# Other batches and other rows for the scattered dV stores of an attention backward kernel

## The chip, the core and the metric

The kernel runs on one core of a Trainium2 chip. The metric is the device time in microseconds (us) of one execution, as the median of several. The core has five engines that compute or issue (TensorE, here PE; VectorE, DVE; ScalarE, ACT; GpSimd, POOL; SyncE, SP) and sixteen DMA engines that move data between the core's memory and the device's. "Engine 4" and the like below always means one of these sixteen.

## The reference

Forward and backward pass of grouped-query attention: 32 batches, 32 query heads, 4 key/value heads, 4 query positions, 2048 keys, head size 128, bfloat16. Returned are the output and the gradients of q, k and v.

```python
B, Hq, Hkv, Sq, Sk, D = 32, 32, 4, 4, 2048, 128

def _fwd_reference(q, k, v):
    k = jnp.repeat(k, Hq // Hkv, axis=1)
    v = jnp.repeat(v, Hq // Hkv, axis=1)
    scores = jnp.einsum("bhqd,bhkd->bhqk", q, k) * D ** -0.5
    p = _softmax(scores, axis=-1)
    return jnp.einsum("bhqk,bhkd->bhqd", p, v)

def reference(q, k, v, grad_out):
    out, vjp = jax.vjp(_fwd_reference, q, k, v)
    return (out, *vjp(grad_out))
```

## The kernel before

One batch is one step of work: 4 heads of keys times 32 query rows (8 query heads by 4 positions) fill the 128 partitions. K, V, dK and dV of a batch are each held in two tiles ("rows") of 128 partitions by 4096 elements, two heads in each; K's tiles and the second tiles of the outputs are 128 elements longer, for q, grad_out, the output and dq. There are 20 such tiles (slots), which loads and stores share.

The whole order of work is written out by hand in the text `PLAN`: four characters name a unit (which operation, which part, where, which tile), and `emit` turns each unit into instructions in that order; nothing reorders them. Within a batch: loads of K and V (L245), transposes of them on PE (L260) and copies out of PSUM by ACT or DVE (L226, L228), scores (L274), minimum and exponential (L279, L283), dop on POOL (L290), transposes of the probabilities, output (L312) and dV (L334) on PE, its copies to the slots (L340), then dP, dS, dQ and dK in the same way. Batches overlap in the plan.

SP issues every plain load (L245) and store (L350; the last pieces of batch 31 L346) in the plan's order. A plain transfer of 128 rows puts 8 rows on each of the 16 DMA engines; each row is one packet of 8192 or 8448 bytes.

Five of the 32 stores of dV's first tile go another way. For a batch in `SPREAD` (L23) SP leaves the store out (L349), and POOL issues it as indirect DMAs ("scatter", L201), in pieces of rows (`PIECES`, L24). This stands behind qp of the next batch (L291 to L299). An indirect DMA of n rows uses as many engines as the largest divisor of n up to 16, one engine after the other from where the last indirect DMA left off: 2 rows lie on two engines, 126 on fourteen with nine rows each. A store of 3 words at the start (L205) moves that place to engine 3, so the 2 rows fall on engines 3 and 4 and the 126 on all the others; 13 words after the last batch (L299) bring it round to 0. Every piece has an output tensor of its own, and the host puts the pieces into dV.

The slot of a scattered tile is written again by the dV copies of batch b+2 (L340).

Of the kernel before, what the change touches and what calls it, by code (L numbers as in the profile page):

```python
# [16 lines left out]
ROW = 2 * 16 * P  # L17
# [2 lines left out]
SLOTS, E_TILES, DS_TILES = 20, 2, 2  # L20
TILES = dict(KT=8, VT=7, ET=2, DT=2)

SPREAD = (4, 6, 8, 10, 12)  # L23
PIECES = ((126, 2), (0, 126))  # L24

NAMES = dict(
    a="LK", b="LV", c="QT", d="QTe", e="KT", f="KTe", g="VT", h="VTe", i="S", j="MX", k="EX", l="RC", m="dop", n="qp",
# [141 lines left out]
def kernel(  # L169
# [8 lines left out]
    dv0: bass.AP,  # L178
    dv1: bass.AP,
    spread,  # L180
    turns,
):
    nc = tc.nc
    B, D, C = k0.shape[0], P, 16
# [13 lines left out]
    at = const_pool.tile([P, 1], mybir.dt.int32, name="at")  # L198
    nc.gpsimd.iota(at[:], pattern=[[0, 1]], base=0, channel_multiplier=1)

    def scatter(out, in_):  # L201
        nc.gpsimd.indirect_dma_start(out=out, in_=in_, in_offset=None,
                                     out_offset=bass.IndirectOffsetOnAxis(ap=at[0:in_.shape[0], 0:1], axis=0))

    scatter(turns[0], at[0:3, 0:1])  # L205
    junk = const_pool.tile([P, D], BF16, name="junk")
    slots = [const_pool.tile([P, LONG], BF16, name=f"row{i}") for i in range(SLOTS)]
    tiles = {x: [const_pool.tile([P, 8 * P], BF16, name=f"{x.lower()}_sb{i}") for i in range(n)]
# [6 lines left out]
    T = collections.defaultdict(dict)  # L215
# [17 lines left out]
    def emit(u):  # L233
# [12 lines left out]
        elif name == "QT":  # L246
            ps = t["qtp"] = bank(u)[:, 0:P]
            for j, x in enumerate(("q", "go")):
                nc.tensor.transpose(out=ps.bitcast(BF16)[:, P * j:P * j + P], in_=t[x], identity=ident[:])  # L249
        elif name == "QTe":  # L250
            t["qdt"] = sm_pool.tile([P, 2 * P], BF16, name="qdt_sb", bufs=3)
            copy16(u.where, t["qdt"][:], t["qtp"])
        elif name in ("KT", "VT", "ET", "DT"):
            x, (half, h) = name[0], divmod(i, NH) if name in ("KT", "VT") else (i, None)
            t[name, i] = tiles[name][u.tile]
            ps = t[name + "p", i] = bank(u)
            src = t[x, h] if h is not None else t["e" if x == "E" else "ds"][:]
            src = src.bitcast(FP32).rearrange("p (j d) -> p j d", d=P)
            for j in range(4):
                nc.tensor.transpose(out=ps[:, P * j:P * j + P], in_=src[:, 4 * half + j, :], identity=ident32[:])  # L260
        elif name in ("KTe", "VTe", "ETe", "DTe"):
            copy16(u.where, t[name[:2], i][:], t[name[:2] + "p", i])
        elif name in ("S", "DP"):
            if name == "S" and i == 0:
                t["S"], t["e"] = bank(u, 4), e_sb[u.tile]
            if name == "DP":
                t["DP", i] = bank(u, 2)
                if i == 0:
                    t["ds"] = ds_sb[u.tile]
            out = t["S"][:, 2 * QW * i:2 * QW * i + 2 * QW] if name == "S" else t["DP", i]  # L270
            x, side = ("KT", 0) if name == "S" else ("VT", 1)
            for w in range(2):
                for h, r in enumerate(rows):
                    nc.tensor.matmul(out[r, QW * w:QW * w + QW], lhsT=t["qdt"][:, P * side + 32 * h:P * side + 32 * h + 32],  # L274
                                     rhs=t[x, NH * i + h][:, QW * w:QW * w + QW],
                                     start=True, stop=True, tile_position=(0, 32 * h))
        elif name == "MX":
            t["m"] = sm_pool.tile([P, 1], FP32, name="m")
            nc.vector.tensor_scalar(out=t["e"][:], in0=t["S"], scalar1=-scale, scalar2=None, op0=ALU.mult,  # L279
                                    op1=ALU.min, accum_out=t["m"][:])  # L280
        elif name == "EX":
            t["l"] = sm_pool.tile([P, 1], FP32, name="l")
            nc.scalar.activation(out=t["e"][:], in_=t["S"], func=ACT.Exp, bias=t["m"][:], scale=scale,  # L283
                                 accum_out=t["l"][:])
        elif name == "RC":
            t["rinv"] = sm_pool.tile([P, 1], FP32, name="rinv")
            nc.vector.reciprocal(out=t["rinv"][:], in_=t["l"][:])  # L287
        elif name == "dop":
            t["dop"] = sm_pool.tile([P, D], BF16, name="dop_sb", bufs=2)
            nc.gpsimd.tensor_scalar(out=t["dop"][:], in0=t["go"], scalar1=t["rinv"][:], scalar2=None, op0=ALU.mult)  # L290
        elif name == "qp":  # L291
            t["qp"] = sm_pool.tile([P, D], BF16, name="qp_sb", bufs=2)
            nc.gpsimd.tensor_scalar(out=t["qp"][:], in0=t["q"], scalar1=t["rinv"][:], scalar2=scale, op0=ALU.mult,
                                    op1=ALU.mult)
            if b - 1 in SPREAD:
                for (first, count), piece in zip(PIECES, spread[SPREAD.index(b - 1)]):
                    scatter(piece, T[b - 1]["DV", "out", 0][first:first + count, 0:ROW])
                if b - 1 == SPREAD[-1]:
                    scatter(turns[1], at[0:13, 0:1])  # L299
        elif name == "rs":  # L300
            t["rs"] = sm_pool.tile([P, 1], FP32, name="rs")
            nc.gpsimd.tensor_scalar(out=t["rs"][:], in0=t["rinv"][:], scalar1=scale, scalar2=None, op0=ALU.mult)
        elif name in ("O", "DQ"):
            if i == 0:
                t[name] = bank(u)[:, 0:D]
            xt, x = ("ET", "V") if name == "O" else ("DT", "K")
            left = t[xt, i][:].rearrange("p (j q e) -> p j q e", q=P, e=2)
            for c in range(8):
                j, odd = divmod(c, 2)
                for h, r in enumerate(rows):  # L310
                    right = t[x, h].rearrange("p (j d e) -> p j d e", d=D, e=2)
                    nc.tensor.matmul(t[name][r, :], lhsT=left[:, j, r, odd], rhs=right[:, 4 * i + j, :, odd],  # L312
                                     start=(i == 0 and c == 0), stop=(i == 1 and c == 7), tile_position=(0, 32 * h))
        elif name in ("Oe", "DQe"):
            x, by, to = ("o", "rinv", "DV") if name == "Oe" else ("dq", "rs", "DK")
            t[x] = t[to, "out", 1][:, ROW:LONG]
            if u.where == "A":
                nc.scalar.activation(out=t[x], in_=t[name[:-1]], func=ACT.Copy, scale=t[by][:])
            else:
                nc.vector.tensor_scalar(out=t[x], in0=t[name[:-1]], scalar1=t[by][:], scalar2=None, op0=ALU.mult)  # L320
        elif name == "DL":
            t["dl"] = sm_pool.tile([P, 1], FP32, name="delta")
            nc.vector.tensor_tensor_reduce(out=junk[:], in0=t["o"], in1=t["go"], scale=1.0, scalar=0.0,
                                           op0=ALU.mult, op1=ALU.add, accum_out=t["dl"][:])
        elif name == "DS":
            w = slice(2 * QW * i, 2 * QW * i + 2 * QW)
            nc.vector.scalar_tensor_tensor(out=t["ds"][:, w], in0=t["DP", i], scalar=t["dl"][:], in1=t["e"][:, w],  # L327
                                           op0=ALU.subtract, op1=ALU.mult)
        elif name in ("DV", "DK"):
            i, g = divmod(i, 2)  # L330
            acc = t[name, i, g] = bank(u, 2)
            moving, still = ("e", "dop") if name == "DV" else ("ds", "qp")
            for h in (2 * g, 2 * g + 1):
                nc.tensor.matmul(acc[:, QW * (h % 2):QW * (h % 2) + QW], lhsT=t[still][rows[h], :],  # L334
                                 rhs=t[moving][rows[h], QW * i:QW * i + QW], start=True, stop=True,
                                 tile_position=(32 * h, 0))
        elif name in ("DVe", "DKe"):
            i, g = divmod(i, 2)
            copy = nc.scalar.copy if u.where == "A" else nc.vector.tensor_copy
            copy(out=heads_of(t[name[:2], "out", g])[:, :, QW * i:QW * i + QW],  # L340
                 in_=t[name[:2], i, g].rearrange("p (h c) -> p h c", h=2))
        elif name == "SK" and i in LAST:
            g, first, runs, n = LAST[i]
            part = lambda row: (row[:, 0:ROW].rearrange("p (h c) -> p h c", h=2)[:, :, first:first + n] if runs == 2
                                else row[:, first:first + n])
            nc.sync.dma_start(out=part(dk_r[g][b]), in_=part(t["DK", "out", g]))  # L346
        elif name in ("SV", "SK"):
            n = LONG if i else ROW
            if not (name == "SV" and i == 0 and b in SPREAD):  # L349
                nc.sync.dma_start(out=(dv_r if name == "SV" else dk_r)[i][b], in_=t["D" + name[1], "out", i][:, 0:n])  # L350
# [48 lines left out]
```

## Time and profile before

| what | before |
|---|---|
| time, median of 3 runs | 668.98 us (667.71 to 670.45) |
| the profiled execution | 667.87 us, its span 665.2 us |
| busy: PE, DVE, ACT, POOL | 605.3, 570.6, 568.6, 51.0 us |
| data moved | 273.96 MB in 38652 packets, 412 GB/s over the span |
| share of the DMA engines' time | SP's queue 96.6%, POOL's 1.9%, instruction fetch 0.6% and 0.1% |
| POOL's indirect DMAs | 10 of rows, 2 of words; issue 0.86 to 1.05 us each |
| scatter, from issue to landing | 5.6 to 12.1 us, median 9.3 |

The span runs from the first to the last instruction. Busy time is that of the engine itself. A DMA is seen in two ways: as an instruction that issues it, and as packets that the sixteen engines move; "landing" is the last of the 16 increments of its semaphore. q1 is SP's queue, q0 POOL's, q8 and q14 fetch instructions.

### The profile page before, as it was taken

To read this page: it belongs to the slowest core of one execution; us is meant where nothing else is said; L and a number is where in the kernel's file an instruction comes from. 1 tells how busy PE (TensorE), PEld (TensorE's weight loads), DVE (VectorE), ACT (ScalarE), POOL (GpSimd) and SP (SyncE) were. 2 spreads that over 40 slices of the span, in tenths; PEclk is the share of its full clock that TensorE was granted. 3 is DMA by queue.
4 is the path that set the end of the run, shared out by engine and by line. 5 is a ranking of instruction groups with operands and counts; after the bars stand their busy time and mean duration, and the time that the engine had idled before them with its cause. 6 is when DMAs were issued, how large, how long until landed. Compare 5 with 4: busy or idle time off the path is not lost.

```text
span 665.2 us, 20671 instructions
## 1 busy us (share of the span) xinstructions
PE 605.3 (91%) x8768; PEld 399.3 (60%) x8768; DVE 570.6 (86%) x736; ACT 568.6 (85%) x802; POOL 51.0 (8%) x115
## 2 busy tenths in 40 slices
PE   6998999999998999989999998997999988897993
PEld 5665566666665666656556665655656565565651
DVE  1988899999998899979898988887889988897893
ACT  3897899999998899979888998886988888887894
POOL 1000000101010010200000000000000000000000
PEclk9999999999999999989999999999999999999998
DMA  9999999999999999999999999999999999999967
GB/s 352 419 425 422 424 399 424 416 423 421 397 425 422 424 422 419 425 413 424 422 424 424 426 423 424 425 425 424 424 423 423 421 422 417 417 421 421 377 286 308
DMA packets 38652, 273.96 MB, mean 412 GB/s; under 512 B 4512, under 2 KB 4512, under 8 KB 6560
## 3 DMA queue, kind: packets, MB, share of 16 engines
q1 hardware_dynamic: 37536, 267.40, 96.6%
q0 software_dynamic: 1024, 5.24, 1.9%
q8 instruction: 68, 1.11, 0.6%
q14 instruction: 24, 0.20, 0.1%
HBM read 136.31 MB, written 136.31 MB: 410 GB/s over the span
## 4 chain that ended last, share of the span: by engine, by line
PE 45%; DMA 41%; ACT 5%; DVE 4%; issue 3%; SPq 0%; DVEq 0%; ACTq 0%
DMA row<-in_k_dram 38%; PE psum L260 23%; PE psum L334 10%; PE psum L312 6%; PE psum L274 6%; ACT row L340 4%; DMA row<-in_v_dram 4%; DVE vt_sb L228 3%; ACT e_sb L283 1%; DVE ds_sb L327 0%; DVE row L340 0%; DVE e_sb L279 0%; PE psum L249 0%; ACT dt_sb L226 0%; SPq L245 0%
## 5 line engine op out<-in xcount | busy, mean ns | idle before, releaser
L340 ACT CAST row<-psum 128x1024 bf16<-128x1024 f32 x292 | 289.9, 1023 | 27.2 <-PE psum L334 23.2
L260 PE MATMUL psum<-ident,row 128*128 128x128 f32 x2048 | 289.5, 283 | 25.1 <-DMA row<-in_k_dram 17.8
L260 PEld LDWEIGHTS psum<-ident,row 128*128 128x128 f32 x2048 | 224.8, 143 | 90.7 <-issue 30.5
L340 DVE CAST row<-psum 128x1024 bf16<-128x1024 f32 x220 | 264.8, 1217 | 7.2 <-PE psum L334 5.0
L226 ACT COPY kt_sb<-psum 128x512 f32<-128x512 f32 x190 | 110.2, 599 | 16.9 <-PE psum L260 16.6
L226 ACT COPY vt_sb<-psum 128x512 f32<-128x512 f32 x160 | 92.0, 602 | 35.8 <-PE psum L260 35.1
L327 DVE SCALAR_TENSOR_TENSOR ds_sb<-psum,delta,e_sb 128x1024 bf16<-128x1024 f32 x64 | 82.1, 1283 | 11.8 <-PE psum L274 7.0
L334 PE MATMUL psum<-ds_sb,qp_sb 32*128 32x512 bf16 x512 | 76.8, 383 | 3.4 <-ACT row L340 1.0
L279 DVE TENSOR_SCALAR_CACHE_REDUCE e_sb<-psum 128x2048 bf16<-128x2048 f32 x32 | 73.3, 2292 | 5.7 <-PE psum L274 5.7
L228 DVE COPY vt_sb<-psum 128x1024 bf16<-128x1024 bf16 x96 | 60.8, 685 | 13.7 <-PE psum L260 13.4
L334 PE MATMUL psum<-e_sb,dop_sb 32*128 32x512 bf16 x512 | 69.7, 384 | 2.2 <-issue 1.4
L283 ACT ACTIVATE e_sb<-psum,m 128x2048 bf16<-128x2048 f32 x32 | 64.0, 2000 | 0.2 <-DVE e_sb L279 0.2
L290 POOL TENSOR_SCALAR dop_sb<-row,rinv 128x128 bf16<-128x128 bf16 x32 | 19.4, 607 | 582.1 <-DVE rinv L287 508.4
L228 DVE COPY kt_sb<-psum 128x1024 bf16<-128x1024 bf16 x66 | 44.9, 683 | 21.4 <-PE psum L260 21.0
L260 PE MATMUL psum<-ident,ds_sb 128*128 128x128 f32 x256 | 41.9, 286 | 9.1 <-DVE vt_sb L228 6.6
L312 PE MATMUL psum<-row,dt_sb 128*32 128x128 bf16 x2048 | 43.7, 222 | 5.9 <-issue 5.3
L334 PEld LDWEIGHTS <-qp_sb 32*128 32x128 bf16 x512 | 19.4, 91 | 46.1 <-issue 42.6
L274 PE MATMUL psum<-vt_sb,qdt_sb 128*32 128x512 bf16 x512 | 40.0, 381 | 4.3 <-issue 4.2
L312 PEld LDWEIGHTS <-dt_sb 128*32 128x32 bf16 x2048 | 30.9, 95 | 21.6 <-issue 20.7
L260 PEld LDWEIGHTS psum<-ident,ds_sb 128*128 128x128 f32 x256 | 26.9, 140 | 26.6 <-DVE vt_sb L228 15.7
L226 ACT COPY dt_sb<-psum 128x512 f32<-128x512 f32 x63 | 38.4, 611 | 4.2 <-PE psum L260 4.1
L312 PEld LDWEIGHTS <-et_sb 128*32 128x32 bf16 x2048 | 30.3, 95 | 13.6 <-ACT et_sb L226 11.9
(32 smaller groups left out, 318.4 us busy)
## 6 DMA issues: line engine op xcount, KB each, us to landing
out_dram<-row SPq DMA_DIRECT2D x63, 1056.0 KB, 19.8
row<-in_k_dram SPq DMA_DIRECT2D x62, 1056.0 KB, 17.9
row<-in_v_dram SPq DMA_DIRECT2D x62, 1024.0 KB, 20.3
out_dram<-row SPq DMA_DIRECT2D x58, 1024.0 KB, 20.2
row<-in_v_dram SPq DMA_DIRECT2D x4, 512.0 KB, 9.4
out_dram<-row SPq DMA_DIRECT2D x3, 512.0 KB, 8.2
row<-in_k_dram SPq DMA_DIRECT2D x2, 544.0 KB, 5.3
row<-in_k_dram SPq DMA_DIRECT2D x2, 512.0 KB, 4.5
```

Source lines behind the costliest of these rows:

```text
L226: nc.scalar.copy(out=out.bitcast(FP32), in_=in_)
L228: nc.vector.tensor_copy(out=out, in_=in_.bitcast(BF16))
L260: nc.tensor.transpose(out=ps[:, P * j:P * j + P], in_=src[:, 4 * half + j, :], identity=ident32[:])
L274: nc.tensor.matmul(out[r, QW * w:QW * w + QW], lhsT=t["qdt"][:, P * side + 32 * h:P * side + 32 * h + 32], rhs=t[x, NH * i + h][:, QW * w: ...
L279: nc.vector.tensor_scalar(out=t["e"][:], in0=t["S"], scalar1=-scale, scalar2=None, op0=ALU.mult, op1=ALU.min, accum_out=t["m"][:])
L283: nc.scalar.activation(out=t["e"][:], in_=t["S"], func=ACT.Exp, bias=t["m"][:], scale=scale, accum_out=t["l"][:])
L290: nc.gpsimd.tensor_scalar(out=t["dop"][:], in0=t["go"], scalar1=t["rinv"][:], scalar2=None, op0=ALU.mult)
L312: nc.tensor.matmul(t[name][r, :], lhsT=left[:, j, r, odd], rhs=right[:, 4 * i + j, :, odd], start=(i == 0 and c == 0), stop=(i == 1 and c ...
L327: nc.vector.scalar_tensor_tensor(out=t["ds"][:, w], in0=t["DP", i], scalar=t["dl"][:], in1=t["e"][:, w], op0=ALU.subtract, op1=ALU.mult)
L334: nc.tensor.matmul(acc[:, QW * (h % 2):QW * (h % 2) + QW], lhsT=t[still][rows[h], :], rhs=t[moving][rows[h], QW * i:QW * i + QW], start=Tr ...
L340: copy(out=heads_of(t[name[:2], "out", g])[:, :, QW * i:QW * i + QW], in_=t[name[:2], i, g].rearrange("p (h c) -> p h c", h=2))
```

## The change

Other batches are scattered, and their rows are cut otherwise. Batches 4, 13 and 18 are stored as 120 rows on fifteen engines from engine 5 on (8 each), and 8 rows on engines 15 and 0 to 6 (1 each): engine 4 takes one row. Batches 7 and 23 are stored as 85 rows on engines 15 and 0 to 3 (17 each), 34 rows on engines 7 and 8 (17 each), and 9 rows on engines 9 to 15, 0 and 1 (1 each). Between the pieces stores of words move the place to the wanted engine. There are still five scattered stores of 128 rows; indirect DMAs become 23 (12 of rows, 11 of words), and the word store at the start of the kernel is gone. The scratch for their descriptors grows from 256 to 512. `PLAN`, the computation and SP's other transfers are the same, but SP now leaves out the stores of these batches.

```diff
-SPREAD = (4, 6, 8, 10, 12)
-PIECES = ((126, 2), (0, 126))
+TO_ONE = ((5, 120), (15, 8))
+TO_SEVEN = ((15, 85), (7, 34), (9, 9))
+SPREAD = {4: TO_ONE, 7: TO_SEVEN, 13: TO_ONE, 18: TO_ONE, 23: TO_SEVEN}
+
+def shares(n):
+    return max(k for k in range(1, 17) if n % k == 0)
+
+def pieces():
+    at, out = 0, []
+    for b, move in SPREAD.items():
+        row = 0
+        for engine, n in move + ((0, 0),) * (b == max(SPREAD)):
+            turn = (engine - at) % 16
+            if turn:
+                out.append((b, None, turn))
+            if n:
+                out.append((b, row, n))
+            row, at = row + n, engine + shares(n) if n else 0
+    return out
...
-    scatter(turns[0], at[0:3, 0:1])
...
-            if b - 1 in SPREAD:
-                for (first, count), piece in zip(PIECES, spread[SPREAD.index(b - 1)]):
-                    scatter(piece, T[b - 1]["DV", "out", 0][first:first + count, 0:ROW])
-                if b - 1 == SPREAD[-1]:
-                    scatter(turns[1], at[0:13, 0:1])
+            for (of, row, n), piece in zip(pieces(), spread):
+                if of == b - 1:
+                    scatter(piece, at[0:n, 0:1] if row is None else T[of]["DV", "out", 0][row:row + n, 0:ROW])
...
-    nc = _bacc.Bacc("TRN2", target_bir_lowering=False, num_devices=1, dynamic_dma_scratch_size=256)
+    nc = _bacc.Bacc("TRN2", target_bir_lowering=False, num_devices=1, dynamic_dma_scratch_size=512)
```

More of the change, by code (lines that the diff above doesn't have):

```diff
@@ L180 @@
     spread,
-    turns,
 ):
@@ L385 @@
         args.append(nc.dram_tensor(f"out_{i}_dram", shape, dt, kind="ExternalOutput").ap())
-    spread = [[nc.dram_tensor(f"dv0_{b}_{first}_dram", (count, ROW), _mybir.dt.bfloat16, kind="ExternalOutput").ap()
-               for first, count in PIECES] for b in SPREAD]
-    turns = [nc.dram_tensor(f"turn_{n}_dram", (n, 1), _mybir.dt.int32, kind="ExternalOutput").ap() for n in (3, 13)]
+    spread = [nc.dram_tensor(f"piece_{i}_dram", (n, 1 if row is None else ROW),
+                             _mybir.dt.int32 if row is None else _mybir.dt.bfloat16, kind="ExternalOutput").ap()
+              for i, (b, row, n) in enumerate(pieces())]
     with _tile.TileContext(nc) as tc:
-        kernel(tc, *args, spread, turns)
+        kernel(tc, *args, spread)
     r = _run(nc, [arrays], core_ids=[0])
@@ L393 @@
     dv0 = dv0.copy()
-    for b in SPREAD:
-        for first, count in PIECES:
-            dv0[b, first:first + count] = _np.asarray(r.results[0][f"dv0_{b}_{first}_dram"])
+    for i, (b, row, n) in enumerate(pieces()):
+        if row is not None:
+            dv0[b, row:row + n] = _np.asarray(r.results[0][f"piece_{i}_dram"])
     shape = (32, 32, 4, 128)
```

## The prediction

> **What bounds the kernel now.** I read the page first: how busy the transfers are, and which queue holds them.
>
> ```profile
> DMA  9999999999999999999999999999999999999967
> GB/s 352 419 425 422 424 399 424 416 423 421 397 425 422 424 422 419 425 413 424 422 424 424 426 423 424 425 425 424 424 423 423 421 422 417 417 421 421 377 286 308
> q1 hardware_dynamic: 37536, 267.40, 96.6%
> q0 software_dynamic: 1024, 5.24, 1.9%
> q8 instruction: 68, 1.11, 0.6%
> ```
>
> The sixteen DMA engines are full until the last three slices, and SyncE's queue q1 fills them. So the time is transfer work, unless the work is spread unevenly. The second view is the chain that ended last, in order of time.
>
> ```profile
> 353.24 1.25 PE psum L260 x8
> 354.79 19.83 DMA row<-in_k_dram
> 374.69 19.83 DMA row<-in_k_dram
> 394.58 20.91 DMA row<-in_k_dram
> ...
> 559.45 20.46 DMA row<-in_k_dram
> 579.98 20.44 DMA row<-in_k_dram
> 600.55 1.94 PE psum L260 x16
> ```
>
> From 355 us each batch waits for the landing of K, 20.5 us after the one before. Before that GpSimd's dop follow each other every 18.86 us (156.74, 175.60), the pace of the computation. The last K lands at 600.4; some 52 us of computation and the last stores follow. A transfer has landed when all 16 engines have done their share, so the slowest engine counts, not the mean.
>
> Third, the single packet records of the trace. They give start, length, size and queue, but not the engine. A packet starts 3 to 4 ns before the one ahead of it on the same engine ends (8 KB packets last 309 ns, those of 8,448 B 319), and every engine runs q1's transfers in the same order. That is enough to put them into 16 lanes. Counted from 20 to 600 us of the span:
>
> ```
> lanes                             q1 rows done   lag at one late landing, us
> 6 without 16 KB fetches           1790 to 1801   among the first seven, 0 to 3.4
> 1 of the two with 5 scattered rows    1800       among the first seven, 0 to 3.4
> 8 with 16 KB fetches              1766 to 1780   6.5 to 10.9
> the other with 5 scattered rows       1761       12.7
> ```
>
> The lag is that of each of the 16 increments of one transfer's semaphore, at 593 us. Three classes appear. Seven lanes lead. Eight carry all the instruction fetches (68 of 16 KB, mean 0.97 us, eight or nine on a lane). One is last: its stores take on average 25 ns longer a row (848 rows, 21.0 us in all; 38 ns between 120 and 330 us, 16 ns after 330), on no other lane. A row costs 0.31 us (starts 305.8 or 315.4 ns apart). At the end fifteen lanes finish the final store within 0.2 us and one 2.33 us later. This slow lane is never idle for more than 0.2 us in all up to 600 us, and works alone at the end: **its own total work is the time of the kernel**, and the others have room.
>
> **The change, part by part.** A plain store puts 8 rows on each engine. Before, five scattered stores put 1 row on each of positions 3 and 4 and 9 on the rest. That fits the trace: each time two lanes take one row and fourteen nine. Both of those lanes have no 16 KB fetches; one leads, one is the slow lane. Over five stores after the change, row counts follow from the number of words and rows of each piece (the diff's own rule, which the 126 rows on 14 lanes bear out):
>
> ```
> position      before  after   difference in us at 0.31
> 4                5       3    -0.6
> 3                5      61    +17.4
> 0, 1, 15        45      63    +5.6
> 2               45      61    +5.0
> 7, 8            45      58    +4.0
> 5, 6            45      27    -5.6
> 9 to 14         45      26    -5.9
> ```
>
> Seven positions gain rows, eight lose them, one stays: the sizes of the three classes in the trace. The records don't say which lane is which position, only that the slow one is 3 or 4; I take it as 4 and come back to it.
>
> *Slow lane.* Two rows less: **-0.6 us**, and this is the sum's only term on the path. The relief also comes later (at batches 4, 7, 13, 18, 23 instead of 4 to 12): by 290 us 20 rows less have been taken away, so the lane lags up to 6 us more there and K is waited for earlier than 355 us. It costs nothing at the end, for the lane's queue holds work all along and all relief falls before the last loads.
>
> *Other lanes.* In rows at 600 us: fetch lanes 1766 to 1780 plus 18 or 19; lanes without fetches 1790 to 1801 minus 13 to 18, thus 1774 or more; slow lane 1763. They stay ahead of it, so 0 us. Lane 3 is the close one: 1800 - 56 = 1744, plus what it lost by being in front. It was idle for 2.67 us (9 rows), and had 7.4 us (24 rows) more in long packets than another lane without fetches, mostly just after it had run out of work. With both it reaches 1776, with none 1744. I take 1776, since a loaded lane no longer runs ahead into an empty queue.
>
> *GpSimd.* One scatter now:
>
> ```profile
> 157.75 0.37 POOL L293 TENSOR_SCALAR qp_sb<-row,rinv 128x128 bf16<-128x128 bf16 x1
> 158.44 0.94 POOL L202 DMA_INDIRECT dv_dram<-row,at  x1 [0.31 <-issue]
> 159.69 1.00 POOL L202 DMA_INDIRECT dv_dram<-row,at  x1 [0.30 <-issue]
> 175.60 0.60 POOL L290 TENSOR_SCALAR dop_sb<-row,rinv 128x128 bf16<-128x128 bf16 x1 [14.91 <-DVE rinv L287]
> ```
>
> 12 issues become 23 (12 of rows, 11 of words), 1.25 us each: 5.0 us in a batch with four, 6.2 with five, 7.5 with six, in place of 2.5. Behind them on GpSimd stands the next dop (L290), for which PE's dV matmuls wait; it has 14.9 us of idle ahead of it, so at least 9.9 stay. Nothing is moved past SyncE's queue: five of its stores are left out, as before, others by number. Words are 4 B; each packet takes 9 ns.
>
> *The tile's next writer.* VectorE and ScalarE write the same tile again for batch b+2 and wait for the scatter. Before, they came 18.7 us after the first scatter's issue at the soonest, and the rows had landed 5.3 us or more earlier. A scattered row starts 3.2 to 6.3 us after its issue and alternates with q1's packets: 0.61 us a row. The 34 rows on two engines (17 each) are the fourth issue of batch 7: 3.75 + 4.6 + 16 x 0.61 + 0.3 + 0.9 to the semaphore = 19.3 us, some 0.6 us too late. At batch 23 a batch lasts 20.5 us and nothing waits. Bounds 0 to 2 us, once; the slow lane has some 8 us of queued work more than the leaders then, which hides it. Without that cover it would be the 0.6 us. I take 0. The larger descriptor scratch has no row; the nearest, the issue at 0.86 to 1.05 us whatever the rows, bounds it at 0 to 0.2 us an issue, on GpSimd's idle time: 0.
>
> **Sum:** 667.87 - 0.6 = 667.3 us for the profiled execution (its span is 665.2, 2.7 lie around it). It was 1.1 us below the median of the runs, 668.98, so I predict **668.4 us**.
>
> A page speaks against the change: the Trainium skill, "DMA: Bandwidth & Descriptors", section "Latency and other measured facts", says that DMA engines 7 and 15 are usually slower than the rest. If position 15 were the slow lane, its 18 rows would make 674.6 us. The trace differs: one lane alone is slow, and it took one scattered row of each store, which 7 and 15 did not; so it gets no chance.
>
> **Rivals.**
> - *A, the slow lane gets faster.* Its long stores (38 ns) fall in the stretch with the scatters, 120 to 300 us. If crowded scatters cause them and 16 ns is the lane's own, 293 rows x 22 ns = 6.5 us go, and the next lanes (1774 to 1776) become last: 14 rows, 4.3 us, **664.7 us**. Against it: 22 ns were there from 40 to 120 us, before any scatter, and 46 ns between 300 and 310 us, after the last.
> - *B, lane 3 becomes the last.* Place: position 3, 56 rows more. It decides once fewer than 19 of the 33 lost rows come back (1763). Price with none back: 1761 - 1744 = 17 rows, +5.3 us, **674.3 us**; with the idle 9 alone 8 rows, 671.5. For it: part of its long packets stand behind its seven 8 KB instruction fetches (queue q14), and such stay. Against it: the other lane with seven fetches lost 1.2 us more than its neighbours, not 7.
> - *C, the change misses its lane:* the slow one is position 3 after all, or the pieces fall on other engines. 56 rows on it: 668.98 + 17.4 = **686 us**. Against it: the match of the classes' sizes, 7, 8 and 1.
>
> **How the numbers follow.** Forecast 0.60, A 0.16, B 0.18, C 0.06. 0.5% is 3.3 us, about what a measurement of this kernel can tell from no change (its three runs differ by 0.4%). A is faster. Of B 0.15 lies above 672.3 and with C makes slower 0.21; the forecast and the rest of B make 0.63 for no change. The range leaves out C and the ends of A and B: 664.5 to 673.5 us. The forecast's own range is 666.5 to 670.5, the spread of the runs with the stall of up to 2 us.
>
> **What would show it.** The last increments of the final store still come from one lane, some 2 us behind the rest; late landings spread from about 5 us of lag to 12, with the two groups now together; the K waits on the chain begin before 355 us and still follow at 20.5 us; q0 keeps 640 packets of 8 KB; GpSimd's idle ahead of the next dop stays above 9 us. I am wrong if the final store's lanes end together (A), if the lag at 593 us grows beyond 15 us (B, C), or if VectorE waits for a scatter for more than 2 us.

## The result, and the profile after

The changed kernel takes 697.71 us (median of 6 runs, 695.71 to 698.32) beside 669.72 us before: a ratio of 1.042, 95% interval 1.0388 to 1.0453, some 28 us slower. 668.4 us had been forecast, with 673.5 as the upper end. The profiled execution took 697.62 us, its span is 695.7.

From the page of the changed kernel: DMA throughput in 40 slices, and the shares of the chain that ended last. The last line is the same row of the kernel before.

```profile
GB/s 348 419 422 425 414 412 421 417 366 423 421 376 297 346 396 422 424 423 399 421 424 425 421 424 416 416 424 423 424 422 394 360 237 388 424 421 424 334 247 309
...
PE 70%; issue 10%; ACT 6%; DVE 6%; DMA 5%; POOL 1%; SPq 0%; DVEq 0%; ACTq 0%
...
PE 45%; DMA 41%; ACT 5%; DVE 4%; issue 3%; SPq 0%; DVEq 0%; ACTq 0%
```

The same bytes move as before, but throughput now has two holes: around slice 12 (209 to 226 us, down to 297 GB/s) and slice 32 (557 to 574 us, 237 GB/s). Before, transfers made up 41% of the chain; now they are 5%, and 10% is "issue", time in which the engine on the chain waited for nothing that the profile shows. Waits for K are 1% of the chain, where they were 38%. The computation itself has become late, and the transfers wait for it.

The waits of the changed kernel (engine, line, what it waited for: total us, times, longest):

```profile
POOL piece_dram L218 <- issue: 36.5, 23, 15.3
...
DVE row L353 <- DMA piece_dram<-row,at: 21.8, 2, 12.4
DVE row L333 <- issue: 18.8, 5, 4.3
ACT row L353 <- DMA piece_dram<-row,at: 18.7, 2, 10.8
```

Two kinds of stall show. Twice (batches 7 and 23) VectorE and ScalarE stand some 10 us before they may write a row tile, because a scattered piece of it has not landed; TensorE stands with them. And five times, once per scatter, VectorE stands about 4 us ahead of the scaling of the output (L333) with no releaser in sight.

**The first stall.** GpSimd's timeline at batch 7 (start, duration, instruction, in brackets the idle time before it):

```profile
184.06 0.95 POOL L218 DMA_INDIRECT piece_dram<-at  x1 [0.31 <-issue]
185.31 1.10 POOL L218 DMA_INDIRECT piece_dram<-row,at  x1 [0.30 <-issue]
186.72 0.87 POOL L218 DMA_INDIRECT piece_dram<-at  x1 [0.30 <-issue]
202.26 1.08 POOL L218 DMA_INDIRECT piece_dram<-row,at  x1 [14.67 <-issue]
```

Words, 85 rows, 3 words; then 14.67 us of nothing, with no semaphore behind it; then the 34 rows, and at 203.65 the 9 rows. GpSimd goes on just after the 85 rows have landed (16.4 us after their issue, at 201.7). In all five such pauses of these runs the 34 rows are issued 0.6 us after the 85 have landed. The chain of waits shows what that does:

```profile
187.59 14.67 issue
...
203.65 14.38 DMA piece_dram<-row,at
...
218.10 1.24 DVE row L353
```

The 9 rows land at 218.0 us; VectorE's copy into the same tile had been ready since 208.7. Batch 23 repeats it: 85 rows issued at 521.72, the 34 rows at 539.34.

**The second stall.** TensorE's timeline of the changed kernel at batch 4:

```profile
121.09 0.77 PE L325 MATMUL psum<-row,et_sb 128*32 128x128 bf16 x40
122.06 0.29 PE L325 MATMUL psum<-row,et_sb 128*32 128x128 bf16 x5 [0.21 <-issue]
122.81 0.29 PE L325 MATMUL psum<-row,et_sb 128*32 128x128 bf16 x5 [0.46 <-issue]
...
124.25 0.29 PE L325 MATMUL psum<-row,et_sb 128*32 128x128 bf16 x6 [0.45 <-issue]
...
126.41 0.63 PE L347 MATMUL psum<-e_sb,dop_sb 32*128 32x512 bf16 x3 [0.84 <-issue]
```

GpSimd's timeline at the same time, the first and the last of its four issues:

```profile
120.84 1.07 POOL L218 DMA_INDIRECT piece_dram<-at  x1 [0.32 <-issue]
...
124.69 0.88 POOL L218 DMA_INDIRECT piece_dram<-row,at  x1 [0.30 <-issue]
```

Before, TensorE did the same 64 short matmuls of the output in one go, beside a scatter of two issues:

```profile
158.69 1.13 PE L312 MATMUL psum<-row,et_sb 128*32 128x128 bf16 x64
```

In the changed kernel 40 of them go through at the usual pace. From 1.0 us after GpSimd's first issue the rest come about five at a time, every 0.73 us, until 0.8 us after the end of its last issue. That is 0.15 us a matmul in place of 0.018, and VectorE waits for the last of them.

### The profile page after: what moved, and what is told of

The parts are those of the page before. It is cut to its first block, busy times and chain, and to the rows that moved or that the text cites. A ratio compares the mean times of both kernels' runs of the same rounds, so it can differ in the third digit from the quotient of the medians.

```text
span 695.7 us, 20685 instructions
## 1 busy us (share of the span) xinstructions
PE 619.3 (89%) x8768; PEld 405.9 (58%) x8768; DVE 572.0 (82%) x736; ACT 568.4 (82%) x802; POOL 61.2 (9%) x126
## 4 chain that ended last, share of the span: by engine, by line
PE 70%; issue 10%; ACT 6%; DVE 6%; DMA 5%; POOL 1%; SPq 0%; DVEq 0%; ACTq 0%
PE psum L275 36%; PE psum L347 15%; PE psum L325 10%; PE psum L289 9%; ACT row L353 5%; DMA piece_dram<-row,at 4%; DVE vt_sb L243 4%; POOL piece_dram L218 1%; DMA row<-in_k_dram 1%; ACT e_sb L298 1%; DVE ds_sb L340 1%; DVE row L353 1%; PE psum L264 0%; DVE e_sb L294 0%; ACT dt_sb L241 0%
## 5 line engine op out<-in xcount | busy, mean ns | idle before, releaser
L353 DVE CAST row<-psum 128x1024 bf16<-128x1024 f32 x220 | 265.1, 1219 | 29.9 <-DMA piece_dram<-row,at 21.8
L347 PE MATMUL psum<-ds_sb,qp_sb 32*128 32x512 bf16 x512 | 78.4, 389 | 3.4 <-ACT row L353 1.0
L325 PE MATMUL psum<-row,et_sb 128*32 128x128 bf16 x2048 | 41.5, 222 | 10.0 <-issue 10.0
L347 PEld LDWEIGHTS <-dop_sb 32*128 32x128 bf16 x512 | 16.5, 91 | 56.4 <-issue 47.8
L325 PE MATMUL psum<-row,dt_sb 128*32 128x128 bf16 x2048 | 47.5, 239 | 2.2 <-issue 1.6
L325 PEld LDWEIGHTS <-et_sb 128*32 128x32 bf16 x2048 | 32.0, 95 | 27.2 <-issue 15.5
L289 PE MATMUL psum<-vt_sb,qdt_sb 128*32 128x512 bf16 x512 | 43.0, 409 | 4.3 <-issue 4.2
L325 PEld LDWEIGHTS <-dt_sb 128*32 128x32 bf16 x2048 | 34.3, 103 | 19.4 <-issue 18.5
```

## The experiments

In what follows the *room wait* is GpSimd's pause between the pieces of batches 7 and 23, and the *bursts* are TensorE's matmuls in fives. Each kernel was timed beside the kernel before on the same chip; ratios are to it.

**1. More descriptor scratch.** Another small pool gives up one buffer to make space for it.

```diff
-            t["qdt"] = sm_pool.tile([P, 2 * P], BF16, name="qdt_sb", bufs=3)
+            t["qdt"] = sm_pool.tile([P, 2 * P], BF16, name="qdt_sb", bufs=2)
-    nc = _bacc.Bacc(..., dynamic_dma_scratch_size=512)
+    nc = _bacc.Bacc(..., dynamic_dma_scratch_size=1024)
```

> The changed kernel with a descriptor scratch of 1024 in place of 512 (and qdt in two buffers in place of three, which makes the room). Theory W (GpSimd waits for room for descriptors ahead of the 34-row pieces): the idle of 14.7 us ahead of the fourth issue of batches 7 and 23 falls to 0.3 us, the dV copies of batches 9 and 25 no longer wait 12 us, and the time comes to 668 to 671 us, near the kernel before. Rival L (17 rows on seven engines make those engines late, whoever issues them): the gap goes but the time stays above 685 us. Rival P (the lower granted clock, 0.956, is a cause of its own): time above 685 us at a clock near 0.956.

679.75 us, ratio 1.0174 (1.0111 to 1.0237), above the 668 to 671 of theory W. GpSimd's timeline of this kernel at batch 7, with the 85 and the 34 rows:

```profile
185.45 1.09 POOL L218 DMA_INDIRECT piece_dram<-row,at  x1 [0.30 <-ACT row L353]
...
188.01 1.08 POOL L218 DMA_INDIRECT piece_dram<-row,at  x1 [0.30 <-issue]
```

And two of its waits:

```profile
DVE row L333 <- issue: 26.4, 5, 7.2
POOL piece_dram L218 <- issue: 6.8, 22, 0.3
```

The room wait is gone with nothing else of the scatter changed, and with it every wait of VectorE for a piece. 18 us come back (16.5 by the ratios). The granted clock rises from about 0.955 to 0.965 with it and the time falls below 685 us, so neither L nor P came about. The bursts stay, and where five or six issues now follow each other they last longer, up to 7.2 us.

**2. No pieces on seven engines,** all five batches as 120 and 8 rows; and **3.** only batch 23 as 85, 34 and 9 rows.

```diff
-SPREAD = {4: TO_ONE, 7: TO_SEVEN, 13: TO_ONE, 18: TO_ONE, 23: TO_SEVEN}
+SPREAD = {4: TO_ONE, 7: TO_ONE, 13: TO_ONE, 18: TO_ONE, 23: TO_ONE}
...
+SPREAD = {4: TO_ONE, 7: TO_ONE, 13: TO_ONE, 18: TO_ONE, 23: TO_SEVEN}
```

> All five batches 4, 7, 13, 18, 23 as 120 + 8 rows, scratch 512: the deep pieces are gone, engine 4 keeps 5 rows as before. Theory W: no long idle between GpSimd's issues, 667 to 671 us. Rival: that other batches and a later relief of engine 4 cost by themselves: 675 us or more.

> 85, 34 and 9 rows at batch 23 alone, the other four as 120 + 8. Theory W: one wait of some 15 us on GpSimd in place of two and about half of the loss, 680 to 686 us. If only the wait at batch 7, where the computation sets the pace, costs time: 668 to 672 us; if only that at batch 23: about 697 us.

677.96 us (ratio 1.0133, 1.0093 to 1.0174) and 689.18 us (1.029, 1.0245 to 1.0335). Without those pieces there is no room wait; with them once, one, of 15.5 us, and VectorE waits 12.2 us for a piece. So one such batch costs 11.2 us and the second, in the changed kernel, another 8.5. In both kernels the bursts remain (23.6 and 20.8 us of VectorE's idle time), and both are above the range of theory W.

**4. The same, one engine earlier,** which puts 45 scattered rows on engine 4 and 5 on engine 3.

```diff
-TO_ONE = ((5, 120), (15, 8))
+TO_ONE = ((4, 120), (14, 8))
```

> As the kernel with all five batches as 120 + 8 rows, but every piece starts one engine earlier, so that engine 3 takes 5 rows and engine 4 takes 45. If engine 4 is the one slow lane and its own work sets the time: 40 rows of 0.31 to 0.33 us more on it, 12 to 13 us over that kernel, 680 to 684 us, and the last store ends on one lane over 10 us behind the rest. If engine 3 is the slow lane: 12 us less than that kernel or bounded by the next lane, 660 to 667 us. If no single engine sets the time: the same within 2 us.

685.15 us (1.026, 1.0211 to 1.0308), 7.2 us above experiment 2. Which of the two engines is the slow one is told by direction: it is 4. The price of a row on it is not told. 40 rows at 0.31 us are 12.4 us, but experiment 2, from which the 7.2 are counted, has its time from the bursts (transfers are 1% of its chain, here 22%), and beside the kernel before, with 5 rows on engine 4 as well, the 40 rows and the bursts together cost some 16 us.

**5 and 6. Bursts alone.** The kernel before, with one issue more ahead of each scatter: 16 words, or 16 rows of 512 bytes. The rows stay on their engines.

```diff
             if b - 1 in SPREAD:
+                scatter(turns[2 + SPREAD.index(b - 1)], at[0:16, 0:1])
...
+                scatter(turns[2 + SPREAD.index(b - 1)], T[b - 1]["DV", "out", 0][0:16, 0:256])
```

> The kernel before, with one store of 16 words (one on each engine, so the place in the round of engines stays) ahead of each of its five scatters: 3 issues in place of 2, the same rows on the same engines, the same batches, the smaller descriptor scratch. Theory (issues slow TensorE): from 1.0 us after the first issue to some 0.8 us after the end of the third, TensorE's output matmuls come in fives every 0.73 us, as in the changed kernel; VectorE stands some 3 us ahead of the output's scaling, five times; of the 8.3 us that five scatters of four issues cost, some 5 are paid: 674 us. Rival (what is left of the loss without the waits for descriptor room is rows on engines and choice of batches): no bursts, 669 to 670 us.

> As the kernel with 16 words ahead of each scatter, but 16 rows of 512 bytes from the row tile in place of the 16 words. Theory (any third issue does it): the same bursts and 674 us. Rival (the stores of words do it, whose packets are of 4 bytes): no bursts, TensorE's 64 output matmuls in 1.1 us as before, 669 to 670 us.

677.64 us (1.0115, 1.0082 to 1.0148) and 674.22 us (1.0089, 1.0047 to 1.0132). TensorE in the kernel with the 16 short rows:

```profile
163.48 0.77 PE L313 MATMUL psum<-row,et_sb 128*32 128x128 bf16 x40
164.45 0.29 PE L313 MATMUL psum<-row,et_sb 128*32 128x128 bf16 x5 [0.20 <-issue]
...
165.94 0.29 PE L313 MATMUL psum<-row,et_sb 128*32 128x128 bf16 x5 [0.45 <-issue]
```

The same picture, brought into the kernel before by one issue of almost no bytes. So the bursts come with the issues, not with other rows or engines, and words are not needed for them.

**7 and 8. The scatters moved,** to the batch whose rows they store. GpSimd then waits for the last dV copy and issues the rows some 8 us sooner (150.75 in place of 158.44 us in experiment 9; 12 us at batch 4 in experiment 7), where TensorE has transposes and matmuls of 512 columns. Words that stand first in a series do not wait for the copy and are still issued beside short matmuls. First with the pieces of experiment 2, then with the changed kernel's pieces and the scratch of 1024.

```diff
-                if of == b - 1:
+                if of == b:
```

> All five scatters as 120 and 8 rows, four issues each, but queued on GpSimd behind the same batch's qp and not the next one's, so that they start when the last dV copy of the batch is done, some 9 us sooner, while TensorE has transposes and matmuls of 512 columns. Theory (issues slow TensorE's 64 short output matmuls): these take 1.1 us again, VectorE's idle time of 4 to 6 us ahead of the output's scaling is gone, 668 to 670 us; if the longer matmuls suffer as well, up to 674. Rival (the remaining loss is rows and batches): 677 to 678 us, as with the scatters where they were.

> The changed kernel with its pieces, the doubled descriptor scratch (1024) and the scatters queued in the same batch. Theory (two costs, the wait for room and TensorE's slowed matmuls, and nothing else): 667 to 670 us, no wait of VectorE for a scatter. Rival (one of the seven loaded engines is last, or the scatters themselves cost): 675 to 680 us.

670.9 us (1.0022, 1.0004 to 1.0041) and 672.39 us (1.0036, 1.0012 to 1.0061). VectorE's wait for the output's matmuls in the second of the two:

```profile
DVE row L333 <- issue: 1.5, 6, 0.3
```

From 26.4 us to 1.5: the bursts are gone from the output's matmuls but for one pause of up to 0.3 us behind the first words, and of the 28 us some 2.4 are left.

**9. Place alone:** the kernel before with its two issues moved the same way; **10. the fourth corner:** the changed kernel, scratch 512, scatters moved.

> The kernel before, its five scatters of two issues queued behind the same batch's qp, some 9 us sooner; nothing else. Theory (two issues cost TensorE nothing at either place): 668 to 671 us, a ratio of 1.000 with its interval about it. Rival (the place itself gains or costs): off by more than 2 us.

> The changed kernel with its descriptor scratch of 512 and only the place of the scatters moved, to the same batch: the fourth corner beside the changed kernel (both costs), the doubled scratch (TensorE's bursts alone) and both together (neither). Theory (the wait for room is a cost of its own): GpSimd stands some 14.7 us between the third issue and the 34 rows at batches 7 and 23, now ahead of the next dop; dop comes some 8 to 10 us late twice, 686 to 692 us, no bursts in the output matmuls. Rival (the wait hurt only because VectorE needed the tile): 671 to 675 us.

The place alone gives 670.19 us (1.0011, 1.0 to 1.0023), so some 0.7 of the 2.4 us may be its own (the interval begins at no change). The fourth corner gives 675.56 us (1.0091, 1.007 to 1.0113); the rival said 671 to 675 and the theory 686 to 692, so the rival came nearer. GpSimd there:

```profile
169.56 0.87 POOL L218 DMA_INDIRECT piece_dram<-at  x1 [0.30 <-issue]
183.95 1.09 POOL L218 DMA_INDIRECT piece_dram<-row,at  x1 [13.53 <-issue]
...
186.25 0.62 POOL L305 TENSOR_SCALAR dop_sb<-row,rinv 128x128 bf16<-128x128 bf16 x1
```

The wait is still 13.5 us long and makes the next dop some 10 us late, as expected; but with two delays of 10 us the kernel is only about 6 us slower than before. The four corners:

| | scatters at their old place | moved |
|---|---|---|
| scratch 512 | 697.71 us, 1.042 | 675.56 us, 1.0091 |
| scratch 1024 | 679.75 us, 1.0174 | 672.39 us, 1.0036 |

The two costs do not add: with the bursts there, the room wait is worth 18 us, without them 3.2; the bursts (with what the place adds) are worth 22 and 7.4. The four were not all timed on the same chip; by the ratios it is 16.5 and 3.7, 22 and 9.2. A reason that fits is in the next table. It is argued from these rows and was not tested by itself. Delay is VectorE's idle time at the output's scaling without a releaser plus its waits for a piece; DMA is the transfers' share of the chain.

| kernel | delay, us | ratio | DMA |
|---|---|---|---|
| before | 0 | 1 | 41% |
| 16 short rows ahead | 14.8 | 1.0089 | 16% |
| 16 words ahead | 15.3 | 1.0115 | 15% |
| 3 words first (see below) | 15.3 | 1.0103 | 19% |
| all 120 and 8 | 23.6 | 1.0133 | 1% |
| rows first, scratch 1024 (see below) | 24.9 | 1.0141 | 1% |
| scratch 1024 | 26.4 | 1.0174 | 3% |
| seven engines once | 20.8 + 12.2 = 33.0 | 1.029 | 3% |
| changed kernel | 18.8 + 21.8 = 40.6 | 1.042 | 5% |

Before, batches from 355 us on take 20.5 us where the computation needs 18.86: some 1.6 us of room in each of 12. A delay of the computation first uses this up: 15 us of delay cost 6 to 8. (By this alone they would cost nothing; why they cost half is open.) With the transfers' share at 1 to 5% the room is gone: from 26.4 to 40.6 us of delay, 14.2 more, the time grows by 16 to 18 us.

**11 to 15. What sets the bursts off.** All at the old place. Issues in order, W words and R rows, and what TensorE's 64 matmuls did:

| kernel | issues | 64 matmuls | time, ratio |
|---|---|---|---|
| before | R2 R126 | 1.13 us | |
| words behind | R2 R126 W16 | 1.13 us | 668.43 us, 0.9999 (0.9986 to 1.0011) |
| 126 rows first | R126 R2 | 1.13 us | 668.37 us, 1.0006 (0.9987 to 1.0026) |
| 2 words first | W2 R2 R126 W14 | 1.13 us | 669.88 us, 1.0022 (1.0004 to 1.004) |
| 3 words first | W3 R2 R126 W13 | bursts | 677.19 us, 1.0103 (1.0067 to 1.0139) |
| 16 words ahead | W16 R2 R126 | bursts | 677.64 us, 1.0115 |
| changed pieces, rows first, scratch 1024 | R120 W11 R8 W and R85 W3 R34 R9 W | bursts | 680.33 us, 1.0141 (1.0087 to 1.0195) |

> The kernel before, with a store of 16 words behind each of its five scatters: issues of 2 rows, 126 rows, 16 words. Theory (three issues in a row slow TensorE whatever stands first): bursts of five matmuls from 1.0 us after the first issue, VectorE idle some 3 us ahead of the output's scaling, 673 to 677 us, as with the 16 words ahead. Rival (what is issued first decides: 16 packets or 5 to 14 words slow TensorE, 2 rows don't): no bursts, 669 to 671 us.

> The kernel before with its two row pieces the other way round: 126 rows (14 engines) first, then the 2 rows; two issues as before. Theory (a wide first issue holds TensorE back, and the issues behind it keep it so): bursts from 1.0 us after the first issue to some 0.8 us after the end of the second, about 2 us, five times; 670 to 673 us. Rival (only words or short packets ahead do it): the 64 matmuls in 1.1 us, 669 to 670 us.

> The kernel before with four issues in each scatter, at the old place: 2 words, 2 rows, 126 rows, 14 words; the rows on the same engines. Theory (it is decided by how many engines the first issue reaches: TensorE has 40 matmuls at hand, and what it takes up next is held back while an issue to many engines is written): nothing stalls, 669 to 671 us. Rival (a store of words ahead of rows slows TensorE): bursts from 1.0 us on as in the changed kernel, 675 to 678 us.

> As the kernel with 2 words, 2 rows, 126 rows and 14 words, but 3 and 13 words. Theory (stores of words ahead of the rows hold TensorE back from three words on, as 3 words did at batch 13 with the doubled scratch): bursts from 1.0 to some 4 us, 675 to 678 us. Rival (words ahead of 2 rows are harmless unless they reach all engines): no bursts, 669 to 671 us.

> The changed kernel with the doubled scratch, the scatters at their old place, and each store of words that stood ahead of a batch's rows issued behind the rows of the scatter before, so that 120 or 85 rows come first; the same pieces on the same engines, the same number of issues. Theory (what is issued first decides, and rows first are harmless): TensorE's 64 output matmuls in 1.1 to 1.6 us, VectorE's idle time of 7 us ahead of the output's scaling gone, 670 to 673 us, as with the scatters moved to the same batch. Rival (four to six issues at this place slow TensorE in any order): bursts, 678 to 681 us.

TensorE with 126 rows issued first, from 158.66 us:

```profile
158.91 1.13 PE L312 MATMUL psum<-row,et_sb 128*32 128x128 bf16 x64
```

Every simple rule for the trigger fell in turn: not three issues in a row (R2 R126 W16 is harmless), not the breadth of the first issue (126 rows on 14 engines are harmless, 3 words on 3 engines are not), not words ahead of rows (with 120 rows first TensorE stops 1.0 us after their issue, before the words behind them are issued). What the harmless ones share, and the others lack, is not found; it stays open. Two observations weaken a rule by the form of the issues. The same 5 words, first at batch 4 with a scratch of 512, go with 64 matmuls in 1.38 us in experiment 7 and in 1.13 in experiment 10. And one profiled execution stands behind each row, while the runs spread: 671.24 to 680.78 us with 3 words first, and with 126 rows first two of ten at 672.0 and 672.3 beside eight up to 670.28. Something that differs from build to build or from run to run is an untested rival.

Two of these kernels show the room wait again, with the scratch of 256. With 2 words first, GpSimd stands 2.7 to 5.4 us ahead of the 14 words; with 3 words first, 3.7 to 5.1 us ahead of the 13:

```profile
166.05 0.88 POOL L202 DMA_INDIRECT turn_dram<-at  x1 [3.47 <-issue]
```

It goes on about 0.5 us after the first words of the series have landed. TensorE's 64 matmuls are over by then.

**16 and 17. A version to beat both.** Scratch 1024; pieces of 2 and 126 rows at batches 4, 6, 8, 10, 12 and 16; at batch 14 once 76 rows on engines 15, 0, 1 and 2, 46 on 7 and 8, 6 on 9 to 14. Engine 4 is relieved of 15 rows more than before. In 16 all scatters are moved to their own batch, in 17 only that of batch 14, and all words are issued behind rows.

```diff
+TO_TWO = ((3, 2), (5, 126))
+TO_SIX = ((15, 76), (7, 46), (9, 6))
+SPREAD = {4: TO_TWO, 6: TO_TWO, 8: TO_TWO, 10: TO_TWO, 12: TO_TWO, 14: TO_SIX, 16: TO_TWO}
```

> A version meant to beat both: scatters in the same batch, scratch 1024, the row pieces of before (2 and 126 rows) at batches 4, 6, 8, 10, 12 and 16, and once, at batch 14, 76 rows on engines 15, 0, 1, 2, 46 on 7 and 8, 6 on 9 to 14. Theory (the slow engine 4 and then the eight with instruction fetches set the end, as the lags at 593 us say): engine 4 loses 15 rows more than before (4.7 us), the eight some 6 (1.9 us), the loaded six gain 12 to 16 (up to 5 us of their room): 664 to 667 us. Rival (the computation's pace with some waits sets it, and no lane has the room that the lags show): 669 to 673 us.

> The version with 76, 46 and 6 rows once, at batch 14, but with the pieces of 2 and 126 rows at their old place again (2 rows first) and all words issued behind rows; only batch 14 is issued in its own batch. Theory (the relief of the engines is worth some 2 to 3 us, and the sooner issues of the five early batches cost that at the start, where the third interval of dop grew from 22.8 to 25.8 us): 666 to 668 us. Rival (the computation's own pace sets the time once the engines are relieved): 668 to 670 us.

668.51 us (0.999, 0.9976 to 1.0004) and 667.72 us (0.9984, 0.997 to 0.9997). The second is as fast as the kernel before or faster by up to 2 us; 664 to 667 us had been hoped for in 16. The waits for K on the chain of 16 behind the first load, four where there were twelve (the profiled execution, 671.52 us, is the slowest of its 12 runs):

```profile
235.23 24.41 DMA row<-in_k_dram
259.70 22.13 DMA row<-in_k_dram
...
522.21 19.83 DMA row<-in_k_dram
542.10 21.30 DMA row<-in_k_dram
```

Transfers fall from 41 to 14% of the chain in 16 and to 32% in 17, and the computation takes their place. So the relief of the engines shows on the chain, but hardly in the time.

## Why the prediction was wrong

- **The failed step** is this one of the change part by part: "The larger descriptor scratch has no row; the nearest, the issue at 0.86 to 1.05 us whatever the rows, bounds it at 0 to 0.2 us an issue". An issue was taken to cost its 1.25 us whatever had been issued before. Measured: 14.67 us before the 34 rows (13.53 with the scatters moved), none with twice the scratch. A count that fits all runs is one entry for every row on the most loaded engine and one for the semaphore, added up over all pieces in flight: words, 85 rows, words, 34 rows are 2 + 18 + 2 + 18 = 40. With the scratch of 256 a sum of 14 passes (2 rows, 126 rows, 16 words) and 16 waits (2 words, 2 rows, 126 rows, 14 words). The Trainium skill, "DMA: Bandwidth & Descriptors", section "Terms", gives a descriptor 16 bytes, in rings that GpSimd's own generation writes; by that a scratch of 512 has 32 entries (an estimate, if its number is the bytes of one ring), too few for 40, 1024 has 64 and 256 has 16. The runs agree. The count itself was found from them and not beforehand.
- *The tile's next writer.* The place was right ("if VectorE waits for a scatter for more than 2 us" was named as what would refute the forecast), the size was not: 0.6 us, bounds 0 to 2, against waits of 9.4 to 12.4 us, since the 34 rows were issued 14.4 us late. "At batch 23 a batch lasts 20.5 us and nothing waits" fell with it.
- *GpSimd's 23 issues hidden in its idle time.* Issues did take about 1.25 us, and with twice the scratch the next dop keeps 17.9 us or more of idle time ahead of it. In the changed kernel the room wait leaves 1.95 us at batch 7 and none at batch 23 (above 9 had been forecast), where dop is some 1 us late. But idle time of GpSimd was taken for free time of the kernel. What else runs during an issue was not asked: TensorE's 64 matmuls right beside it. Between the two kernels with scratch 1024 this is 7.4 us (9.2 by the ratios), a term the sum did not have. The trace of before gave no sign of it, with an issue 0.25 us ahead of those very matmuls.
- *The slow engine's own work is the time.* Not the whole account: 15 rows less on engine 4, 4.7 us of work, gave 0.7 us in experiment 16 and 1.1 in 17, at most 2.0 by the intervals. The computation takes the transfers' place on the chain there, so it was close behind. What took the rest of the 4.7 us is not separated: at 18.86 us a batch the computation had some 20 us of room over the second half (an estimate), enough for all of it. Experiment 4 does not decide it, for its time has the bursts in it. Nor does any record tie position 4, counted from the kernel's first indirect DMA, to a number of an engine, so the prediction's dismissal of 7 and 15 by their numbers was not tested.
- *-0.6 us for two rows less, 0 for the other lanes.* With both costs out of the way the changed kernel's rows stand at 1.0036. The terms are right within some 2 us; the rest, beyond the 0.7 us of the moved place, is not traced to an engine, so a little of rival B may be in it. (The lanes without fetches come to 1790 - 18 = 1772 rows at the least, not 1774, which changes nothing.)
- *Rivals.* A and B did not come about in the changed kernel. C gave 686 us for 56 rows on the slow engine; experiment 4 puts 40 more there than before and takes 685.15, but with bursts that cost 8.8 in experiment 2, so C's price is not tested by it. The rival that came true, a full descriptor scratch, had been costed at 0 and was not made a rival.

## What to carry to other kernels

An indirect DMA costs more than its issue: before cutting a store into pieces, add up the descriptors in flight against the scratch, because GpSimd stands without any semaphore when they don't fit, and everything behind the last piece is late. Place the issues beside long matmuls rather than dense short ones, and see in the trace what TensorE does in the 5 us of a series. And before relieving one limit, read how far the next one is: here some 1.6 us a batch, which is also what hides a new delay.

## What was not expected of the hardware

- GpSimd's issues can slow TensorE: about five short matmuls every 0.73 us instead of one every 0.018 us, from 1.0 us after the first issue to 0.8 us after the last, after some 40 that pass. In the profiled executions it happened in every scatter of some kernels that began beside those matmuls, and in none of others; what decides is open.
- GpSimd stands when descriptors don't fit (13.5 to 15.5 us behind 85 rows, 2.7 to 5.4 us behind 2 or 3 words with the scratch of 256), and goes on about 0.5 us after the piece whose room it needs has landed.
- A stall can be paid for twice. In the windows view of the changed kernel (from and to, length, busy time of PE, PEld, DVE, ACT and POOL, granted clock, DMA share, GB/s) the clock falls to 0.53 in the 14 us with the end of the wait, and TensorE's first matmuls after it are slow: 32 short ones take 1.04 us, where the kernel before has 0.66. The clock falls after bursts too, to 0.51 in the 7 us behind the first series (first line). What this costs by itself was not separated.

```profile
126.00:133.00 7.00, 6.59 (x91) 3.91 (x91) 4.31 (x7) 3.52 (x4) 0.00 (x0) 0.51 1.01 404
198.00:212.00 14.00, 11.50 (x158) 7.89 (x154) 10.22 (x13) 11.61 (x17) 3.16 (x5) 0.98 0.98 369
212.00:226.00 14.00, 6.62 (x94) 3.93 (x94) 5.58 (x8) 3.56 (x5) 0.00 (x0) 0.53 0.67 279
226.00:240.00 14.00, 13.64 (x173) 9.22 (x174) 13.21 (x17) 13.25 (x21) 1.21 (x3) 1.00 0.97 347
```

The 32 matmuls, in the changed kernel after the stall and in the kernel before:

```profile
221.43 1.04 PE L325 MATMUL psum<-row,dt_sb 128*32 128x128 bf16 x32
123.63 0.66 PE L312 MATMUL psum<-row,dt_sb 128*32 128x128 bf16 x32
```

The transfers' share falls with the stall, from 0.98 to 0.67: a hole that no later slice makes up for.
